# B's projections, dilated attention and A's last queries on 64x64 array tiles in one mode

## The chip, the cores and the metric

One core of a Trainium2 chip. The metric is the device time of one execution in microseconds (us). The experiments ran on three chips (e1 to e4, e5 to e11, e12). The kernel before, timed in the same rounds, took 488.0, 488.2 and 489.4 us on them (medians), so between these three groups the ratios are the safer comparison. Shares, chains and timelines come from one profiled execution of each kernel, whose span is about 2 us shorter than the time reported for it. Ratios are the mean time of one kernel's runs over that of the other's of the same rounds, so they are not quite the ratio of the medians that are quoted beside them.

## The reference, cut to what matters

Two attention blocks over the same `x` (2048 tokens, 1024 wide, 32 heads of 32) are mixed by a gate. A is linear attention. B is softmax attention in which each query sees 8 keys, two tokens apart.

```python
def _B_ref(x, wqkv, wo):
    W, dil = 8, 2
    q, k, v = ...                                  # x @ wqkv, heads of 32
    idx = pos[:, None] - (jnp.arange(W) * dil)     # even queries see even keys only, odd ones odd keys
    logits = einsum(q, k[idx]) * Dh ** -0.5        # masked where idx < 0
    return (softmax(logits) @ v[idx]) @ wo
# out = g * A(x) + (1 - g) * B(x), g = sigmoid((x * gate_w).sum(-1))
```

Tokens are held sorted by parity, so a query needs its own key and the 7 before it of the same parity.

## The kernel before, cut to what the argument touches

The middle stage, from the first projection of B's keys to the first output product, is what the change rewrites. For each of 8 head groups (128 columns, 4 heads) it makes K and Q with 64 dense matmuls of 128x128x512. In between, at fixed positions, it drops the score and PV bursts of the head group before.

```python
# dense: one matmul per k-tile, one PSUM bank per output
nc.tensor.matmul(st["pj"][:], lhsT=W[c // 4][:, kt, (c % 4) * P:(c % 4 + 1) * P],
                 rhs=xT[:, kt, cols], start=(kt == 0), stop=(kt == KT - 1))

def scores(g):            # 4 tiles of 128 keys x 112 or 128 queries, 4 heads each
    for i in range(4):    # contraction 32: one 32-row tile of the array per head
        r = slice(32 * i, 32 * i + 32)
        nc.tensor.matmul(s4[:, i, o:o + w], lhsT=kqts[c][r, 0, k0:k0 + P], rhs=kqts[c][r, 1, q0:q0 + w], ...)
    # exp on ScalarE, times mask on VectorE -> pt
def pv(g):                # 16 full 128x128 weight loads of pt, 33 columns of V (32 + a column of ones)
    nc.tensor.matmul(oB[b][:, tt - 2 * b, i, :], lhsT=pt[:, i * W_ + o:i * W_ + o + P], rhs=V[:, t, c * 4 + i, :], ...)
    # reciprocal and multiply on VectorE -> Ob, then a transposing DMA straight into OBT
...
p_ = 64 + 3 + 512 * g / len(state)          # 36 bursts, spread evenly over the dense matmuls
events.append((p_, lambda g=g: scores(g)))
events.append((p_ + 18, lambda g=g: pv(g)))
```

The output stage then sums A-side products (`pqT` with `WoA`) and B-side products (`OBT` with `WoB`) in one PSUM bank per output part.

The softmax here doesn't subtract the row's maximum and nothing guards it: scores larger than these inputs give would overflow.

## Time and profile before

| | before |
|---|---|
| time, median of 3 | 488.18 us (488.06 to 488.19) |
| TensorE busy, share of the span | 480.5 us, 99% |
| VectorE, ScalarE | 58%, 39% |
| dense matmul 128x512, start to start | 215.8 ns |
| middle stage, from its first dense matmul to the first output product | 153.5 us |
| output stage, from there to the last matmul's start | 110.8 us |

Two lines of the page of the kernel before: busy time of each engine with its share of the span and its instructions, and the chain of waits by engine.

```profile
PE 480.5 (99%) x3444; PEld 227.0 (47%) x3444; DVE 281.0 (58%) x533; ACT 187.4 (39%) x283; POOL 15.9 (3%) x33
...
PE 98%; DMA 1%; SPq 1%; ACT 0%; issue 0%; ACTq 0%
```

The chain is nearly all TensorE: nothing but less or denser TensorE work can shorten this kernel. Now one cycle of attention, from the timeline of the kernel before (start, length, engine, line, operation, count; lengths include about 0.16 us of pipeline after the last start).

```profile
301.78 0.81 PE L339 MATMUL kq_ps<-xT,WkB 128*128 128x512 bf16 x3
...
302.52 0.38 PE L365 MATMUL s<-kqt 32*128 32x128 bf16 x16
...
302.83 1.04 PE L339 MATMUL kq_ps<-xT,WkB 128*128 128x512 bf16 x4
...
303.71 0.56 PE L390 MATMUL oB<-V,PT 128*128 128x33 bf16 x16
...
304.12 0.38 PE L339 MATMUL kq_ps<-xT,WkB 128*128 128x512 bf16 x1
```

Read starts, not lengths. Three dense matmuls from 301.78 are due to end at 301.78 + 3 x 0.216 = 302.43, and the scores begin at 302.52. That is 95 ns of nothing, and 91 ns follow the last score matmul. The scores cost about 0.40 us (302.83 - 302.43) where four rounds of 49 ns, 0.2 us, would do. The PV burst, with no gap before or after it, takes 0.41 us (16 starts, 25.3 ns apart).

### The profile page before, as it was taken

Reading aid. Unit: us, or ns where it says so; the run is one execution under the profiler, and the core shown is the slowest. Engines: PE = TensorE matmul, PEld = TensorE weight load, DVE = VectorE, ACT = ScalarE, POOL = GpSimd, SP = SyncE. Lnnn points to the kernel's source line nnn. Section 1 sums busy time; section 2 is a strip of 40 time slices with the busy share of each in tenths; the row PEclk is TensorE's granted clock in tenths of the full one; section 3 lists DMA queues with packets and bytes.
Section 4 is the critical chain, followed back from the end, with each engine's and each line's share of the span. In section 5 each row is a group of like instructions: output and inputs, shape, how many; then the busy total and the mean of one; then the engine's idle time right before and its main releaser. Section 6 shows DMA issues by size and latency. Waiting matters only on the chain.

```text
span 486.2 us, 8390 instructions
## 1 busy us (share of the span) xinstructions
PE 480.5 (99%) x3444; PEld 227.0 (47%) x3444; DVE 281.0 (58%) x533; ACT 187.4 (39%) x283; POOL 15.9 (3%) x33
## 2 busy tenths in 40 slices
PE   7999999999999999999999999999999999999997
PEld 4444444445444444444444445544445444444444
DVE  1766689992429999995466556656654596000000
ACT  1333321111633333332666666666565332212121
POOL 3000001411000000000000000000000000000000
PEclk9999999999999999999999999999999999999999
DMA  8999960001522223354011161111173833111101
GB/s 194 171 291 369 348 207 0 0 1 36 190 76 93 72 71 93 95 158 131 11 30 31 30 121 27 38 30 32 31 172 78 198 88 86 34 43 34 43 33 45
DMA packets 80182, 46.57 MB, mean 96 GB/s; under 512 B 53520, under 2 KB 74128, under 8 KB 80144
## 3 DMA queue, kind: packets, MB, share of 16 engines
q1 hardware_dynamic: 80144, 46.04, 34.9%
q8 instruction: 27, 0.44, 0.4%
q14 instruction: 11, 0.09, 0.1%
HBM read 21.23 MB, written 7.34 MB: 59 GB/s over the span
## 4 chain that ended last, share of the span: by engine, by line
PE 98%; DMA 1%; SPq 1%; ACT 0%; issue 0%; ACTq 0%
PE kq_ps L339 23%; PE d_ps L454 21%; PE p_ps L258 11%; PE g_ps L200 11%; PE pk_ps L152 11%; PE p_ps L296 9%; PE q_ps L296 3%; PE oB L390 3%; PE s L365 2%; PE q_ps L454 1%; DMA WkA<-in_A_wqkv_dram 1%; PE kv_ps L220 0%; PE p_ps L246 0%; SPq L95 0%; SPq L98 0%; SPq L99 0%
## 5 line engine op out<-in xcount | busy, mean ns | idle before, releaser
L375 ACT ACTIVATE PT<-s 128x896 bf16<-128x896 f32 (+1 forms) x72 | 63.0, 926 | 24.5 <-PE s L365 24.5
L339 PE MATMUL kq_ps<-xT,WkB 128*128 128x512 bf16 x256 | 65.3, 379 | 0.0
L339 PE MATMUL kq_ps<-xT,WqB 128*128 128x512 bf16 x256 | 64.8, 379 | 0.0
L376 DVE TENSOR_TENSOR PT<-PT,mask 128x896 bf16<-128x896 bf16 (+1 forms) x72 | 44.6, 623 | 26.6 <-ACT PT L375 26.6
L258 PE MATMUL p_ps<-WvB,xT 128*128 128x512 bf16 x256 | 57.9, 379 | 0.0
L152 PE MATMUL pk_ps<-WkA,xT 128*128 128x512 bf16 x256 | 56.0, 379 | 1.3 <-DMA WkA<-in_A_wqkv_dram 0.8
L454 PE MATMUL d_ps<-WoA,pqT 128*128 128x512 bf16 (+1 forms) x248 | 56.9, 372 | 0.0
L454 PE MATMUL d_ps<-WoB,OBT 128*128 128x512 bf16 (+1 forms) x248 | 56.9, 372 | 0.0
L200 PE MATMUL g_ps<-pk,xrow 128*128 128x512 bf16 x256 | 55.4, 379 | 0.0
L140 DVE TENSOR_SCALAR e<-e 128x512 f32<-128x512 f32 x64 | 28.1, 438 | 41.8 <-ACT e L139 41.8
L459 ACT ACTIVATE osb<-d_ps,omg 128x512 bf16<-128x512 f32 (+1 forms) x31 | 20.9, 673 | 76.5 <-PE d_ps L454 73.7
L296 PE MATMUL p_ps<-WqA,xT 128*128 128x512 bf16 x192 | 43.4, 379 | 0.0
L344 ACT CAST kqt<-kq_ps 128x512 bf16<-128x512 f32 x48 | 28.2, 587 | 31.8 <-PE kq_ps L339 31.6
L152 PEld LDWEIGHTS <-xT 128*128 128x128 bf16 x256 | 24.9, 98 | 32.2 <-issue 1.6
L454 PEld LDWEIGHTS <-pqT 128*128 128x128 bf16 x264 | 25.8, 98 | 29.5
L454 PEld LDWEIGHTS <-OBT 128*128 128x128 bf16 x264 | 25.8, 98 | 29.3
L200 PEld LDWEIGHTS <-xrow 128*128 128x128 bf16 x256 | 25.0, 98 | 30.2
L258 PEld LDWEIGHTS <-xT 128*128 128x128 bf16 x256 | 24.6, 98 | 30.0 <-issue 0.9
L296 PEld LDWEIGHTS <-xT 128*128 128x128 bf16 x256 | 24.3, 98 | 28.5
L139 ACT ACTIVATE e<-pk_ps 128x512 f32<-128x512 f32 x32 | 19.0, 597 | 42.0 <-PE pk_ps L152 42.0
L339 PEld LDWEIGHTS <-WqB 128*128 128x128 bf16 x256 | 22.9, 97 | 24.7
L339 PEld LDWEIGHTS <-WkB 128*128 128x128 bf16 x256 | 22.6, 97 | 24.1
(56 smaller groups left out, 394.1 us busy)
## 6 DMA issues: line engine op xcount, KB each, us to landing
xrow<-in_A_x_dram SPq DMA_DIRECT2D x4, 1024.0 KB, 12.3
out_dram<-osb SPq DMA_DIRECT2D x31, 128.0 KB, 1.9
pqd<-tmp SPq DMA_DIRECT2D x12, 256.0 KB, 2.0
WvA<-in_A_wqkv_dram SPq DMA_DIRECT2D x2, 1024.0 KB, 15.0
WoA<-in_A_wo_dram SPq DMA_DIRECT2D x2, 1024.0 KB, 12.7
WvB<-in_B_wqkv_dram SPq DMA_DIRECT2D x2, 1024.0 KB, 12.5
WqA<-in_A_wqkv_dram SPq DMA_DIRECT2D x2, 1024.0 KB, 9.7
WkB<-in_B_wqkv_dram SPq DMA_DIRECT2D x2, 1024.0 KB, 6.6
```

The lines of the kernel that those rows point to most:

```text
L139: nc.scalar.activation(out=e[:], in_=pj[:], func=ACT.Exp)
L140: nc.vector.tensor_scalar(out=e[:], in0=e[:], scalar1=1.0, scalar2=1e-6, op0=ALU.min, op1=ALU.add)
L152: nc.tensor.matmul(pj[:], lhsT=xT[:, kt, t * P:(t + 1) * P], rhs=WkA[half][:, kt, :], start=(kt == 0), stop=(kt == KT - 1))
L200: nc.tensor.matmul(pj[:], lhsT=xrow[:, t, kt * P:(kt + 1) * P], rhs=pk[:, t, half * 512:(half + 1) * 512], start=(t == 0), stop=(t == NB - 1))
L258: nc.tensor.matmul(st["pj"][:], lhsT=xT[:, kt, t * P:(t + 1) * P], rhs=WvB[half][:, kt, :], start=(kt == 0), stop=(kt == KT - 1))
L296: nc.tensor.matmul(st["pj"][:], lhsT=xT[:, kt, t * P:(t + 1) * P], rhs=WqA[half][:, kt, :], start=(kt == 0), stop=(kt == KT - 1))
L339: nc.tensor.matmul(st["pj"][:], lhsT=W[c // 4][:, kt, (c % 4) * P:(c % 4 + 1) * P], rhs=xT[:, kt, cols], start=(kt == 0), stop=(kt == KT - 1))
L344: (nc.vector.tensor_copy if 0 <= after < 4 else nc.scalar.copy)(out=kqt[:, which, cols], in_=st["pj"][:])
L375: nc.scalar.activation(out=ptv[:, hs], in_=s4[:, hs, 0:W_], func=ACT.Exp, scale=SCALE)
L376: nc.vector.tensor_tensor(out=ptv[:, hs], in0=ptv[:, hs], in1=m[:, None, :].broadcast_to([P, 2, W_]), op=ALU.mult)
L454: nc.tensor.matmul(st["ps"][:, 0:n], lhsT=lhsT, rhs=W[c0 // 512][:, c, c0 % 512:c0 % 512 + n], start=(side == 0 and c == 0), stop=(side == ...
L459: nc.scalar.activation(out=osb[:, 0:n], in_=st["ps"][:, 0:n], func=ACT.Copy, scale=omg[:, tb:tb + 1])
```

## The change

The intent: put everything in the middle stage on 64x64 tiles, so that the array never changes mode. A dense step becomes four matmuls of 64x64x512 on the four tiles. Blocks of 64 keys replace tiles of 128. The two parities lie on the two partition halves. Scores and PV run four at a time. The exp and mask work is nearly halved. Cut to its core:

```diff
+            def quad_units(outputs):        # 4 outputs (K, Q of two parities), 4 slots of 8 steps
+                def step(slot, kt):
+                    for j in range(2):      # output half
+                        for r in range(2):  # row half
+                            o = (slot + 2 * r) % 4
+                            mm(o, r, kt, j, slot < 2)        # 64x64 weights, 512 columns
+                    if kt == KT - 1:
+                        for r in range(2):
+                            o = (slot + 2 * r) % 4
+                            if slot < 2:    # the bank goes to the other row half: a small read orders them
+                                nc.vector.tensor_copy(out=seen[:], in_=banks[o][:, 0:1])
+                            else:
+                                outputs[o][2](banks[o])
+                def evacuate(ps):           # Q twice, each with the other head of a pair zeroed
+                    if which == 0:
+                        nc.scalar.copy(out=kt_[:, par, 512 * hh:512 * hh + 512], in_=ps[:])
+                        return
+                    nc.scalar.activation(out=qz[:, 0, par, :], in_=ps[:], func=ACT.Copy, scale=qsel[:, 0:1])
+                    nc.vector.tensor_scalar(out=qz[:, 1, par, :], in0=ps[:], scalar1=qsel[:, 1:2], ...)
...
+                            nc.tensor.matmul(s2b[64 * par:64 * par + 64, pair, :, o:o + w],
+                                             lhsT=kts[c][r, par, k0:k0 + 64], rhs=qz[r, :, par, ...], ...)
...
+                                nc.tensor.matmul(o2[64 * h:64 * h + 64, par, s_, i, :], lhsT=pt[r, i, o:o + 64],
+                                                 rhs=V[r, m, 4 * c + i, :], ...)
...
-                    nc.sync.dma_start_transpose(out=OBT[:, c, q0:q0 + m * w]..., in_=Ob[0:w, t0:t0 + m]...)
+                        nc.sync.dma_start(out=obd[c][...], in_=Ob[64 * h:64 * h + w, par, sl:sl + k, :])
+                if part:
+                    nc.sync.dma_start_transpose(out=OBT[:, c, :], in_=obd[c][0:S, :])
...
+                p_ = 64 * c + (40, 52, 72, 84, 95)[m // 4]       # scores; PV 14 steps later
...
+            first = [out_part(*p_) for p_ in parts[:3]]          # A sides of 3 parts, then their B sides
+            for k in range(2):
+                for f in first:
+                    f(k)
```

V now goes to its blocks through DRAM, and the projection banks are 4 instead of 2 (6 to 4 in the first stage).

## The prediction

> **What bounds the kernel now.** TensorE: the page has PE busy 480.5 of 486.2 us, and the chain of waits is 98% PE. A dense 128x512 matmul starts every 215.8 ns. From 218 to 374 us B's projections are interrupted 36 times by attention. The trace in order of time: the 16 score matmuls (four at a time, 49 ns a set) have gaps of 95 ns before and 91 ns after them, about 0.42 us in all; the 16 PV matmuls start every 25.3 ns, 0.41 us. Together 0.83 x 36 = 29.8 us. Only this can shrink: dense work keeps its multiply-adds (576 steps of four 64x64 matmuls). VectorE (58%) and ScalarE (39%) are off the chain, so halving their exp and mask work gains nothing by itself.
>
> **What changes, costed.**
> - Dense steps. The Trainium skill, "TensorE: Matmul & The Clock Gate", Part 3, says tiles run concurrently; the trace agrees: 16 matmuls of 32x32x512 started 3.5 ns apart, all done within 0.36 us. A tile's weight load hides behind its running matmul: in the 128x64 products two tiles ran 64 columns every 31.5 ns. I expect 216 to 217 ns per step, +0.6 us over 576.
> - Mode switches. "TensorEngine Tiling (Array Packing)", Key Properties, says a mode change drains the array; the 95 and 91 ns gaps agree. One mode removes 36 x 0.19 = 7 us.
> - Scores: 8 x 18 rounds of four, 49 ns each: 7.1 us.
> - PV: twice the matmuls (1152), four at a time: 288 rounds at the 31.5 ns of the 128x64 product = 9.1 us, against 14.6.
> Attention: 16.2 instead of 29.8 us, -13.6.
>
> **What is given back (estimates).**
> - In-order queues. VectorE must mask, finish O (1.2 us a batch) and clear two Q banks (0.69 us each) before slot 1 of the next quad: about 12 us of work in each 16 us head group, one place late by 0.4 us: 8 x 0.4 = 3 us.
> - End of attention. O of the last group goes to DRAM by small writes, then one 2048x128 transpose, behind two 512x1024 transposes of pqT in the same queue (4.0 us of issue each). Last PV to landing: 1 us VectorE + 0.6 + 4 + 2.2 + 4 + 2.2 + 2 = 16 us. Cover: 18 quad steps, 24 A-side, 7 B-side matmuls = 10.7 us. TensorE idles about 5 us; the clock may drop (same page, Part 1; no idle in this trace shows it), 1 us more.
> - First stage with four banks instead of six, V through DRAM: under 1 us.
>
> Sum: 488.2 - 13.6 + 0.6 + 3 + 5 to 6 = 483; shaded to 481.5, as the positions look tuned.
>
> **Predicted: 481.5 us, 8 in 10 between 474 and 489.** Faster by over 2% (below 478.4): 0.28; within 2%: 0.67; slower: 0.05.
>
> **What would show it.** Quad matmuls: four per 216 ns. No 90 ns gaps around scores. PV bursts of 32 in about 0.25 us. PE idle on q4_ps bank releases, 2 to 4 us in all. One PE gap of about 5 us before the B-side matmul of the last group, released by the OBT transpose; lower granted clock just after.
>
> **What would make it wrong.** If weight loads (no fast load with column tiling) did not hide, steps of 240 ns or more: +14 us. PV starts limited by issue at 12 ns each: +5 us. If the last transpose landed in time: -5 us, faster by 2%. Bank releases on ScalarE later than summed: +3 to 8 us.

## The result, and the profile after

The changed kernel takes 501.25 us (median of 4 runs, 499.13 to 503.78) against 488.19. The ratio is 1.0266, with a 95% interval from 1.0228 to 1.0305: it is slower. Both the size and the direction of the forecast were wrong.

The same two lines of the page of the changed kernel:

```profile
PE 473.5 (95%) x5748; PEld 249.3 (50%) x5748; DVE 280.9 (56%) x605; ACT 167.9 (34%) x267; POOL 25.7 (5%) x88
...
PE 69%; DVE 20%; SPq 3%; ACT 3%; issue 3%; DMA 2%; ACTq 0%; DVEq 0%
```

TensorE is no longer the whole chain: VectorE has 20% of it. (Part of these 20% is the normalisation of A's queries in the first stage, to which the chain goes back from the first small read.) First, TensorE's own work, in the timeline of the changed kernel:

```profile
239.94 1.06 PE L365 MATMUL q_ps<-xT,WkB 64*64 64x512 bf16 x16
240.81 0.41 PE L418 MATMUL s2b<-qz,kt 64*64 64x114 bf16 x16
241.01 0.63 PE L365 MATMUL q_ps<-xT,WkB 64*64 64x512 bf16 x8
241.44 0.43 PE L441 MATMUL o<-V,PT 64*64 64x33 bf16 x30
```

16 small matmuls, four steps, take 240.81 - 239.94 = 0.87 us, so about 216 ns a step. The scores take 0.20 us from start to start, with no gap on either side. Single records of a PV burst show four starts every 31.5 ns. All three are what was predicted. But the stage as a whole lasts 372.30 - 218.68 = 153.6 us, as long as before. What TensorE waited for, from its list of waits (engine, tile, line, what ended the wait; us in total, times, longest):

```profile
PE d_ps L542 <- DMA OBT<-obd: 9.7, 1, 9.7
PE s2b L418 <- DVE qz L400: 5.7, 16, 0.5
PE q_ps L365 <- issue: 1.7, 1, 1.7
...
PE q_ps L365 <- DVE seen L377: 1.2, 2, 0.9
```

**Loss one, in the stage.** The work is 576 x 0.2162 + 7.1 + 9.1 = 140.7 us, so 12.9 us are lost. The last three lines above account for 8.6. That list counts idle time from the end of a matmul, and a start that waited also loses the overlap of about 0.18 us with the matmul before it (the restart, below). Counted from start to start, the 19 waits cost 12.1 us: 8.6 for `qz`, 1.6 for `seen` and 1.9 for the stop. The other 0.8 us is not explained. The commonest wait has its cause in these lines of the timeline:

```profile
235.88 1.27 ACT L399 ACTIVATE qz<-q_ps,qsel 128x512 bf16<-128x512 f32 x2 [0.65 <-PE q_ps L365]
...
236.60 1.41 DVE L400 TENSOR_SCALAR qz<-q_ps,qsel 128x512 bf16<-128x512 f32 x2 [1.01 <-ACT qz L399]
...
238.07 0.35 PE L418 MATMUL s2b<-qz,kt 64*64 64x114 bf16 x12 [0.20 <-DVE qz L400]
```

VectorE sat idle for 1.01 us and started its first copy when ScalarE's first copy (0.69 us) ended, at 236.57. It reads the same PSUM bank. The semaphores in the trace confirm it: VectorE's instruction waits for the one that ScalarE's copy raises, not for the one that TensorE raises. VectorE's own list of waits has this in all 16 places:

```profile
DVE qz L400 <- ACT qz L399: 12.8, 16, 2.7
```

So the three copies in a row, not two pairs side by side, set when the scores can start.

**Loss two, at the end of the stage.** TensorE in the timeline of the changed kernel:

```profile
377.49 1.67 PE L542 MATMUL d_ps<-WoB,OBT 128*128 128x512 bf16 x7
388.89 5.98 PE L542 MATMUL d_ps<-WoB,OBT 128*128 128x512 bf16 x17 [9.73 <-DMA OBT<-obd]
```

The DMA queue in the same timeline (start, and how long the issues held the queue):

```profile
369.54 2.66 SPq L464 DMA_DIRECT2D obd<-Ob  x5
372.30 4.91 SPq L519 DMA_TRANSPOSE pqT<-pqd  x1
377.30 2.17 SPq L464 DMA_DIRECT2D obd<-Ob  x4
379.51 4.58 SPq L519 DMA_TRANSPOSE pqT<-pqd  x1
384.32 2.48 SPq L469 DMA_TRANSPOSE OBT<-obd  x1
```

And the table by stretches of 5 us of the changed kernel (the first line names the columns):

```profile
core 0: us, PE busy (x) PEld busy (x) DVE busy (x) ACT busy (x) POOL busy (x), PEclk, DMA share, GB/s
...
380.00:385.00 5.00, 0.00 (x0) 0.00 (x0) 0.00 (x0) 0.00 (x0) 0.00 (x0) 0.80 0.98 196
385.00:390.00 5.00, 1.11 (x3) 0.43 (x4) 0.00 (x0) 0.40 (x1) 0.00 (x0) 0.50 0.66 130
390.00:395.00 5.00, 5.00 (x17) 1.96 (x16) 0.00 (x0) 1.06 (x3) 0.00 (x0) 0.67 0.16 52
```

The seven B-side products end at 377.49 + 7 x 0.216 = 379.0 and the eighth starts at 388.89: 9.9 us of nothing. The last PV burst had ended at 368.1; then the queue issued small writes, a transpose of pqT, small writes, the other transpose, and only then the transpose that TensorE needs. The granted clock fell to 0.5 in that stretch, and the next 17 products take 394.71 - 388.89 = 5.8 us instead of 3.7. Together that is 12 us, and the output stage takes 122.5 us against 110.8.

**Loss three, once.** TensorE stops for 1.67 us with no releaser ("issue"). The records of the instruction queue show why: in this stage, from 240 us on, one 16 KB fetch of instructions comes every 4.7 us on average (every 10.8 us in the kernel before, which has 1712 matmuls in the stage against 4032). The fetch just before this stop came 7.9 us after the last, behind a 1 MB load of `WoB` and two transposes. The experiments below have eight more such stops. Each ended 2.2 to 2.7 us after a late fetch began, and counted in TensorE's instructions the stops of one kernel lie whole blocks of 16 KB apart (10177 - 6593 = 14 x 256 in e3_both, 7340 - 6572 = 3 x 256 in e7_wob; 45 fetches for 11504 instructions make 64 bytes each). So TensorE had run out of instructions. A long interval alone does not show lateness: near 231 us, before attention is in full swing, TensorE uses a block more slowly, and 7.5 us pass between fetches without a stop.

### The profile page after: what moved, and what is told of

It is laid out like the page before. It is cut to its first block, busy times and chain, and to the rows that moved or that the text cites. A ratio compares the mean times of both kernels' runs of the same rounds, so it can differ in the third digit from the quotient of the medians.

```text
span 498.1 us, 13237 instructions
## 1 busy us (share of the span) xinstructions
PE 473.5 (95%) x5748; PEld 249.3 (50%) x5748; DVE 280.9 (56%) x605; ACT 167.9 (34%) x267; POOL 25.7 (5%) x88
## 4 chain that ended last, share of the span: by engine, by line
PE 69%; DVE 20%; SPq 3%; ACT 3%; issue 3%; DMA 2%; ACTq 0%; DVEq 0%
PE d_ps L542 21%; PE q_ps L365 18%; PE g_ps L201 11%; PE pk_ps L153 11%; DVE qz L400 5%; PE p_ps L276 4%; DVE tmp L141 3%; DVE tmp L293 3%; DVE den L295 3%; DVE tmp L302 3%; ACT qz L399 2%; PE s2b L418 2%; SPq L519 2%; DVE e L140 2%; PE o L441 1%
## 5 line engine op out<-in xcount | busy, mean ns | idle before, releaser
L542 PE MATMUL d_ps<-WoB,OBT 128*128 128x512 bf16 (+1 forms) x264 | 62.6, 382 | 9.7 <-DMA OBT<-obd 9.7
L365 PE MATMUL q_ps<-xT,WkB 64*64 64x512 bf16 x1024 | 70.1, 377 | 0.9 <-DVE seen L377 0.9
L365 PE MATMUL q_ps<-xT,WqB 64*64 64x512 bf16 x1024 | 63.2, 376 | 0.3 <-DVE seen L377 0.3
L542 PE MATMUL d_ps<-WoA,pqT 128*128 128x512 bf16 (+1 forms) x264 | 60.3, 373 | 0.0
L423 ACT ACTIVATE PT<-s2b 128x928 bf16<-128x928 f32 (+4 forms) x40 | 34.2, 855 | 56.2 <-PE s2b L418 56.2
L425 DVE TENSOR_TENSOR PT<-PT,mask 128x928 bf16<-128x928 bf16 (+4 forms) x40 | 23.6, 590 | 34.6 <-ACT PT L423 34.6
L365 PEld LDWEIGHTS <-WqB 64*64 64x64 bf16 x1024 | 33.6, 107 | 16.5 <-issue 0.9
L153 PEld LDWEIGHTS <-xT 128*128 128x128 bf16 x256 | 24.9, 98 | 32.8 <-issue 2.2
L276 PEld LDWEIGHTS <-xT 128*128 128x128 bf16 x256 | 24.7, 98 | 30.0 <-issue 0.9
L365 PEld LDWEIGHTS <-WkB 64*64 64x64 bf16 x1024 | 30.7, 107 | 14.0 <-issue 1.8
L281 ACT CAST tmp<-p_ps 128x512 bf16<-128x512 f32 x32 | 18.7, 589 | 37.4 <-PE p_ps L276 32.6
L312 PEld LDWEIGHTS <-xT 128*128 128x128 bf16 x192 | 18.8, 98 | 22.6
```

The lines of the kernel that those rows point to most:

```text
L153: nc.tensor.matmul(pj[:], lhsT=xT[:, kt, t * P:(t + 1) * P], rhs=WkA[half][:, kt, :], start=(kt == 0), stop=(kt == KT - 1))
L276: nc.tensor.matmul(st["pj"][:], lhsT=xT[:, kt, t * P:(t + 1) * P], rhs=WvB[half][:, kt, :], start=(kt == 0), stop=(kt == KT - 1))
L312: nc.tensor.matmul(st["pj"][:], lhsT=xT[:, kt, t * P:(t + 1) * P], rhs=WqA[half][:, kt, :], start=(kt == 0), stop=(kt == KT - 1))
L365: nc.tensor.matmul(banks[o][64 * j:64 * j + 64, :], lhsT=lhsT(r, kt, j), rhs=rhs(r, kt), start=first and kt == 0, stop=kt == KT - 1, skip_ ...
L423: nc.scalar.activation(out=pt[:, :, 0:W_], in_=s2b[:].rearrange("p a b s -> p (a b) s")[:, :, 0:W_], func=ACT.Exp, scale=SCALE)
L425: nc.vector.tensor_tensor(out=pt[:, :, 0:W_], in0=pt[:, :, 0:W_], in1=mask[:, None, base:base + W_].broadcast_to([P, 4, W_]), op=ALU.mult)
```

## The experiments

Twelve kernels were run. All gave the right result. "Stage" is the middle stage and "output" the output stage, both from the timeline of the one profiled run.

| kernel | time, us | ratio to before, 95% | stage | output |
|---|---|---|---|---|
| before | 488.19 | 1 | 153.5 | 110.8 |
| changed | 501.25 | 1.0266 (1.0228 to 1.0305) | 153.6 | 122.5 |
| e1_evac | 496.07 | 1.0163 (1.0127 to 1.0199) | 145.6 | 125.3 |
| e2_tail | 495.79 | 1.0136 (1.0087 to 1.0184) | 153.0 | 118.2 |
| e3_both | 489.31 | 1.0026 (1.0001 to 1.0051) | 148.3 | 115.3 |
| e4_warm | 500.02 | 1.0243 (1.0213 to 1.0272) | 153.3 | 120.3 |
| e5_cover | 482.16 | 0.9868 (0.984 to 0.9896) | 147.1 | 110.5 |
| e6_dense | 496.74 | 1.017 (1.0147 to 1.0194) | 158.7 | 112.5 |
| e7_wob | 483.01 | 0.989 (0.9869 to 0.9911) | 147.0 | 110.5 |
| e8_all | 480.62 | 0.9848 (0.9823 to 0.9874) | 146.2 | 110.5 |
| e9_pieces | 484.16 | 0.9921 (0.9881 to 0.996) | 146.8 | 110.5 |
| e10_place | 482.81 | 0.9886 (0.985 to 0.9922) | 147.5 | 110.5 |
| e11_swap | 489.88 | 1.0034 (1.0011 to 1.0057) | 146.6 | 117.8 |
| e12_two | 479.03 | 0.9792 (0.9773 to 0.9811) | 144.4 | 110.5 |

The start of the stage wanders from 218.4 to 220.5 us among these profiled runs, with the waits for the first loads of the first stage. In six of them (e2, e3, e4, e5, e7, e12) the clock also stood at 0.5 for 3.4 us near 8 us, and these are the six that start after 219.8. So single spans are not compared below 2 us.

### e1_evac: Q cleared bank by bank

```diff
-                    nc.scalar.activation(out=qz[:, 0, par, :], in_=ps[:], ..., scale=qsel[:, 0:1])
-                    nc.vector.tensor_scalar(out=qz[:, 1, par, :], in0=ps[:], scalar1=qsel[:, 1:2], ...)
+                    for slot in range(2):
+                        if par == 1:
+                            nc.scalar.activation(out=qz[:, slot, par, :], in_=ps[:], ..., scale=qsel[:, slot:slot + 1])
+                        else:
+                            nc.vector.tensor_scalar(out=qz[:, slot, par, :], in0=ps[:], scalar1=qsel[:, slot:slot + 1], ...)
```

> Only the clearing of Q changes: ScalarE makes both masked copies of one Q bank and VectorE both of the other, instead of each engine making one copy of each bank. Theory A (the two engines may not read one PSUM bank together, so VectorE's copies start only after ScalarE's, and TensorE waits for a chain of about 2.1 us where 1.4 us would do): TensorE's waits for VectorE's qz, 5.7 us in 16 waits of 0.24 or 0.47 us, shrink below 1 us, each also saves its pipeline refill of about 0.16 us, and the time falls by 6 to 10 us, to about 491 to 495. Rival B (the placement of the score bursts or the total of VectorE's work sets the wait): the same work in the same place, the waits stay within 1 us of 5.7 us and the time within 2 us of 501.

The timeline of e1_evac, at the same place of a later head group:

```profile
252.08 1.41 DVE L404 TENSOR_SCALAR qz<-q_ps,qsel 128x512 bf16<-128x512 f32 x2 [0.40 <-PE q_ps L365]
252.09 1.27 ACT L401 ACTIVATE qz<-q_ps,qsel 128x512 bf16<-128x512 f32 x2 [0.70 <-ACT kt L397]
```

Two lines of TensorE's list of waits in e1_evac:

```profile
PE d_ps L546 <- DMA OBT<-obd: 13.0, 1, 13.0
PE s2b L422 <- DVE qz L404: 1.5, 7, 0.2
```

The engines now copy side by side, the waits fell from 5.7 to 1.5 us (I had expected under 1), and the stage from 153.6 to 145.6 us. About 2 us of that is the late fetch, which this run did not have; the other 6 are the 4.2 us of waits and their restarts. Theory A held for the stage. The time fell by only 5.2 us, about 1 us short of the range expected: the wait at the end grew from 9.7 to 13.0 us, because TensorE reached the output stage 7.4 us earlier, but the last transpose was issued only 4.1 us earlier (380.20 against 384.32). A gain in the stage is partly given back at a later wait until that wait is gone too.

### e2_tail: the last transpose first

```diff
             for r0 in (512, 1024):
+                nc.vector.tensor_copy(out=pqT[2][:, 0, r0 - 512:r0 - 511], in_=OBT[:, KT - 1, 0:1])
                 nc.sync.dma_start_transpose(out=pqT[2][:, :, r0 - 512:r0], in_=pqd[r0:r0 + 512, :])
```

The added copies make the two large transposes depend on the arrival of `OBT`. Without such a dependency they go ahead of it, as in the changed kernel, where they are written after it too.

> Only the queue order at the end of attention changes: the two 512x1024 transposes of pqT are made to wait for the transpose of the last head group. Theory A (queue order: they stand ahead of it and hold the queue 4.9 and 4.6 us): the one TensorE gap of 9.7 us shrinks to 0 to 1.5 us, the granted clock stays at 1.0, and the time falls by 10 to 12 us, to about 489 to 491. Rival B (the small writes to DRAM, their landing and the transpose itself are the long part): the gap shrinks by less than 4 us.

The wait at the end in TensorE's list of waits of e2_tail:

```profile
PE d_ps L543 <- DMA OBT<-obd: 5.2, 1, 5.2
```

Its DMA queue, from the timeline:

```profile
371.75 6.76 SPq L464 DMA_DIRECT2D obd<-Ob  x9
380.72 1.76 SPq L469 DMA_TRANSPOSE OBT<-obd  x1
385.47 8.04 SPq L520 DMA_TRANSPOSE pqT<-pqd  x2
```

The time fell by 5.5 us, half of what I expected: neither theory alone. The queue order was worth 4.5 us of the wait. The other half is the path itself: nine small writes hold the queue for 6.8 us, the transpose waits 2.2 us for them to land (378.51 to 380.72), and the product that waits for it starts 4.5 us after its issue began. In this profile the clock still fell (the 17 products took 6.1 us), where I had expected it to stay. One of the four timed runs, at a mean clock of 1.0, took 491.31 us, almost what theory A said. No profile fell on it, so how its wait differed is not known.

### e3_both: both edits

> Both edits. If the two losses are separate and add up: 501 less 6 to 10 less 10 to 12, so 479 to 485, faster than the kernel before by 1 to 2%. If they overlap (quads that end earlier leave less cover for the tail), the gain is 3 us or more short of the sum of the two single gains.

489.31 us: 11.9 us gained, where the single gains add up to 10.6. The losses are separate and add up. It still does not beat the kernel before (ratio 1.0026, from 1.0001 to 1.0051), and it missed the 479 to 485 expected because e2_tail gained half of what I expected and e1_evac a little less. A wait of 3.0 us for `OBT` is left.

### e4_warm: the idle stretch filled with useless matmuls

```diff
+            spare = ps_pj.tile([P, 512], F32, name="spare", tag="pj")
+            for i in range(44):
+                nc.tensor.matmul(spare[:], lhsT=xT[:, 0, 0:P], rhs=WoA[0][:, 0, :], start=True, stop=True)
```

> 44 matmuls of no use (9.5 us) are put in the gap before the last B-side products, so that TensorE does not idle there. The result stays right. Theory A (the idle time lets the clock drop, and the products after it run at a lower clock for about 5 us): the granted clock stays at 1.0 and the time falls by about 2 us although nothing useful was added. Rival B (the lower clock costs nothing or comes from something else): same time within 0.5 us, or the clock drops all the same.

In the profiled run the clock stays at 1.0 from 11 us on. The 17 products after the wait:

```profile
389.91 3.84 PE L542 MATMUL d_ps<-WoB,OBT 128*128 128x512 bf16 x17 [0.22 <-DMA OBT<-obd]
```

They take 393.59 - 389.91 = 3.7 us instead of 5.8, and the output stage is 120.3 us against 122.5: 2.2 us less, the whole slow part. In the timed runs the gain is 1.2 us (500.02 against 501.25, with overlapping intervals), so they alone do not settle it. The traces do: the same wait without idling costs nothing afterwards. The Trainium skill, "TensorE: Matmul & The Clock Gate", Part 1, describes this gate: an idle window of about 3.4 us brings half clock until TensorE has been busy for as long. The trace agrees roughly, with 0.5 in a stretch where TensorE hardly ran and 2.2 us lost after it. A shorter stretch was enough, though: 3.0 us of idle time in e3_both brought 3.4 us at half clock, while 2.1 us in e6_dense brought none.

### e5_cover: more independent work ahead of the last transpose

```diff
-            first = [out_part(*p_) for p_ in parts[:3]]
+            AHEAD = 7          # four more banks, free after attention
+            first = [out_part(*p_, *((ps_pj, "pj") if i < 3 else (ps_3, "d3"))) for i, p_ in enumerate(parts[:AHEAD])]
```

This is e3_both with 7 A sides, 12.1 us of matmuls, ahead of the first B side.

> e3_both with the A-side products of seven output parts instead of three ahead of the first B-side product (four more PSUM banks, free after attention): 32 matmuls, 6.9 us more cover for the last transpose. Theory A (what is left of the tail is latency that more independent work hides): the gap of 3.0 us and the dip of the clock vanish, 3 to 4.5 us less than e3_both of the same kind of run, about 485 to 486.5. Rival B (the transpose is held up by other traffic and lands later still): a gap of over 1 us stays.

482.16 us. The wait for `OBT` is gone from the list and the output stage is 110.5 us. Before, that stage held one PV burst of 0.41 us as well, so it is now exactly the dense work of the kernel before. Theory A held. The gain over e3_both, 7.2 us, is more than the 3 to 4.5 expected: 4.8 us of it is the output stage (115.3 to 110.5) and 1.2 us the middle stage, where this run lists 0.9 us of late fetch instead of 1.9. The two profiled runs differ by just 5.5 us. The medians differ by more because three of e5_cover's four runs had a mean clock of 1.0, and none of e3_both's had.

### e6_dense: dense steps back on 128x128, attention left on 64x64

```diff
-                    for j in range(2):
-                        for r in range(2):
-                            mm(o, r, kt, j, slot < 2)
+                    nc.tensor.matmul(st["ps"][:], lhsT=lhsT(kt), rhs=rhs(kt), start=kt == 0, stop=kt == KT - 1)
```

This is e3_both otherwise. It undoes the one mode and nothing of the attention.

> e3_both with the dense steps put back to 128x128 matmuls, attention left on 64x64 tiles. Theory A (the change of mode costs about 95 ns each way, as in the kernel before, and one mode removes it): 40 score bursts and 40 PV bursts, each with 0.19 us of switching, +15 us of TensorE time, less 1.5 to 3 us of waits for the reads that order the halves and the Q banks: 12 to 14 us slower than e3_both, about 501 to 503. Rival B (four matmuls of 64x64 cost more per step than one of 128x128, so the dense steps lose what the switches gain): within 4 us of e3_both.

The timeline of e6_dense around one score burst and one PV burst:

```profile
256.83 1.03 PE L361 MATMUL q_ps<-xT,WkB 128*128 128x512 bf16 x4
257.79 0.40 PE L407 MATMUL s2b<-qz,kt 64*64 64x114 bf16 x16
258.34 0.38 PE L361 MATMUL q_ps<-xT,WkB 128*128 128x512 bf16 x1 [0.16 <-issue]
258.65 0.43 PE L430 MATMUL o<-V,PT 64*64 64x33 bf16 x32
```

The switches are back: 95 ns before the scores (257.69 to 257.79), and 0.55 us from their start to the next dense matmul where one mode needs 0.20. The stage is 158.7 us against 148.3, so 10.4 us longer, although e6_dense has none of e3_both's waits for `qz` and `seen`. The timed runs are 7.4 us slower than e3_both, below the 12 to 14 expected, but far from B's "within 4"; 2.8 us of the stage's loss come back in the output stage (112.5 against 115.3), where the wait for `OBT` is shorter. So the one mode is worth at least 10 us of the stage. It was not the mode that made the changed kernel slow.

### e7_wob, e8_all: the load moved, the first small reads moved

```diff
-            WoB = load_w("WoB", B_wo, 0, "wb")
+            WoB = load_w("WoB", B_wo, 0, "wb", only=(0,)) + load_w("WoB", B_wo, 0, "wc", only=(1,))
```

> e5_cover with the second half of WoB loaded about 256 steps earlier into a buffer that is free by then, out of the stretch in which TensorE waited 1.1 to 1.7 us with nothing that released it. Theory A (TensorE runs dry there because a fetch of its instructions, one every 4.4 us in the quads, stands behind the 1 MB load and the transposes): the gap disappears or falls below 0.3 us, fetches there stay under 6 us apart, 1 to 2 us faster than e5_cover. Rival B (the transposes of pqT alone hold up the fetch): the gap stays at 1 us or more.

483.01 us, no faster than e5_cover. The stop at the old place (0.87 us in the profiled run of e5_cover) is gone, but a new one stands at 299.6 us, behind the load at its new place (issued at 291.5 us), where two fetches came 7.6 us apart. So A's mechanism holds and its gain does not: I had only moved the load, and put 2 MB in a row.

e8_all adds, for the first quad, the small reads on ScalarE:

```diff
-                                nc.vector.tensor_copy(out=seen[:], in_=banks[o][:, 0:1])
+                                (nc.scalar.copy if early else nc.vector.tensor_copy)(out=seen[:], in_=banks[o][:, 0:1])
```

> e7_wob, and the four small reads that order the row halves in the first quad are made by ScalarE, because VectorE is still normalising A's queries there. The waits of 0.9 and 0.3 us on these reads go, with their refills 1.5 us: about 481.5 to 484, 1% faster than the kernel before. If the waits only move to the Q banks of the first quad, which VectorE clears, less than 0.5 us is gained.

480.62 us, 1.5% faster than before, a little better than expected; the waits for `seen` are gone from the list. In its timeline the late fetch is plainer still (two fetches 8.5 us apart):

```profile
294.89 0.81 PE L365 MATMUL q_ps<-xT,WkB 64*64 64x512 bf16 x10
297.44 0.62 PE L365 MATMUL q_ps<-xT,WkB 64*64 64x512 bf16 x6 [1.73 <-issue]
```

TensorE stops in the middle of a dense output, after 10 of 16 matmuls, where no data is awaited.

### e9_pieces, e10_place: two misses

e9_pieces is e8_all with `WoB` in 16 pieces of 128 KB that ScalarE issues over the last four head groups.

```diff
+                    nc.scalar.dma_start(out=WoB[h][:, kt, :], in_=B_wo[kt * P:(kt + 1) * P, 512 * h:512 * h + 512])
+                    events.append((64 * c + (5, 18, 37, 50)[i], wo_event(c, i)))
```

> e8_all with WoB fetched in 16 pieces of 128 KB, spread over the last four head groups and issued by ScalarE at set places, instead of 2 MB at once. Theory A (a fetch of TensorE's instructions is late wherever a big load stands before it): no fetch of the quads comes over 6 us after the one before, no TensorE gap without a releaser in the quads, about 1.5 us faster than e8_all, 479 us. Rival B (the late fetch has another cause): a gap of 0.7 us or more stays. A risk: ScalarE holds back its copies while it waits to issue a piece; then waits for its copies appear on TensorE.

No fetch came over 5.9 us after the one before, and no stop without a releaser is left in the quads: A's mechanism again. But the time rose to 484.16 us: the risk named came true, with 0.9 us of new waits for ScalarE's `PT` in the profiled run. Three of the six timed runs were at 481.7 to 482.8 us, and three at 485.5 to 486.4 with a lower mean clock (0.993). No profile fell on one of the slower three, so what happened in them stays open.

e10_place moves the last score burst of each head group two steps on.

```diff
-                p_ = 64 * c + (40, 52, 72, 84, 95)[m // 4]
+                p_ = 64 * c + (40, 52, 72, 84, 97)[m // 4]
```

> e9_pieces with the last score burst of each head group two dense steps later, so that its mask no longer stands before the clearing of Q on VectorE. The waits for VectorE's qz (1.5 us in 7 waits of 0.2 us) disappear, with their refills about 2.5 us: 476.5 to 478 us, over 2% faster than the kernel before. If they only move to ScalarE or to the bank releases, less than 1 us.

482.81 us, against 476.5 to 478 expected. The waits for `qz` are gone, and 3.0 us in three waits for ScalarE's copies of K appeared: the wait only moved, as the second half of the expectation says.

### e11_swap: each engine still one copy of each bank, in crossed order

```diff
+                    act(0, pa, psa)      # ScalarE on the one bank, VectorE on the other,
+                    dve(1, pb, psb)
+                    act(0, pb, psb)      # then they change
+                    dve(1, pa, psa)
```

> e3_both, but with each engine making one copy of each Q bank, as in the changed kernel, only in such an order that the two are never due on one bank at once (ScalarE begins with the one bank, VectorE with the other, then they change). It tells two readings of e1_evac apart. Theory A (what cost the time was that both engines had to take turns on one bank): the same as e3_both within 1 us, and the stage from the first quad to the first output product within 1 us of its 148.3 us. Rival B (the split of the work by bank did it, for instance because one semaphore wait fewer is on the way): the stage is back near 153 us.

The two engines at the first pair of copies, and TensorE's wait for `qz`, in e11_swap:

```profile
235.65 1.51 ACT L408 ACTIVATE qz<-q_ps,qsel 128x512 bf16<-128x512 f32 x2 [0.65 <-PE q_ps L365]
235.68 1.44 DVE L412 TENSOR_SCALAR qz<-q_ps,qsel 128x512 bf16<-128x512 f32 x2 [0.33 <-PE q_ps L365]
...
PE s2b L434 <- ACT qz L408: 1.9, 7, 0.3
```

VectorE now starts when TensorE releases it. The stage is 146.6 us and the time 489.88, against 148.3 and 489.31 for e3_both. The stage falls outside the 1 us band on the better side, as this run had no late fetch (e3_both listed 1.9 us). The time does not follow, as the wait for `OBT` is 5.8 us against 3.0. The copies and their split between the engines are those of the changed kernel, only never both engines on one bank at once: the gain is there. It was the turns on one bank.

### e12_two: `WoB`'s second half in two pieces

This is e8_all with two issues of 512 KB instead of 1 MB straight after the first.

```diff
+            for i in range(2):
+                events.append((64 * (5 + i) + 46, wo_event(i)))    # ScalarE, 4 k-tiles each
```

> e8_all with the second half of WoB in two pieces of 512 KB, issued by ScalarE in the sixth and seventh head groups at a place where it has nothing due, instead of 1 MB straight after the first half. Theory A (the fetch of instructions was 8.5 us after the one before it because 2 MB stood in front of it): no interval over 6.5 us, no gap without a releaser over 0.5 us, no new waits for ScalarE (two issues instead of sixteen), 1 to 1.7 us faster than e8_all: 479 to 479.6 us. If ScalarE's waits for its own issues cost as much as in e9_pieces, no faster than e8_all.

479.03 us, ratio 0.9792 (from 0.9773 to 0.9811). All that TensorE waits for in e12_two:

```profile
PE s2b L422 <- DVE qz L404: 1.5, 7, 0.2
PE pk_ps L153 <- DMA WkA<-in_A_wqkv_dram: 1.2, 2, 1.1
PE warm L159 <- DVE onesb L110: 1.1, 1, 1.1
PE pk_ps L153 <- DMA xT<-in_A_x_dram: 0.5, 1, 0.5
```

From 240 us on the longest interval between fetches is 5.6 us, and no stop without a releaser is left in the stage. The time is in the range expected. This version beats both kernels. The interval reaches past 0.98, so "faster by over 2%" stays unclear, "faster" does not.

## Why the prediction was wrong, point by point

- **Bound, dense steps, mode, scores, PV: right.** The dense step measured 216 ns (predicted 216 to 217), scores 0.20 us a burst without gaps, PV four per 31.5 ns. e6_dense shows that the mode is worth 10 us or more. The fear about weight loads did not come true. e12_two's stage is 144.4 us against 153.5 before: of the 13 us predicted as TensorE work saved, 9 can be had.
- **The step that failed first: "one place late by 0.4 us: 8 x 0.4 = 3 us".** It measured 8.6 us, of the 12.9 lost in the stage. The prediction had dense matmuls wait for VectorE to release banks, and no such wait is listed; the scores waited for `qz`. I let ScalarE and VectorE clear Q side by side. They share a bank and took turns, so the scores were late in 16 places, not 8, and each wait cost a restart of about 0.18 us as well. e1_evac took about 6 us off the stage with this alone, and e11_swap shows that the turns were the cause. The Trainium skill has the rule behind this: "PSUM — Partial Sum Buffer", section "PSUM bank collisions raise a hardware error", has any two engines kept off one bank on the same partitions, reads included. I had not looked it up for two readers. No run here lets them collide; what the trace shows is VectorE kept waiting for ScalarE's copy, 12.8 us of its idle time in 16 places.
- **The small reads that order the row halves were not costed at all** in the sum. They cost 1.2 us of waits (1.6 us from start to start), only in the first quad, where VectorE was still normalising A's queries. e8_all removed them.
- **The second failed step: "TensorE idles about 5 us; the clock may drop ..., 1 us more".** The mechanism was right, in order, queue and clock. The size was 9.9 and 2.2 us. From the last PV to landing I added up 16 us; it took about 20.8 (368.1 to 388.9). The cover was right: 10.9 us of work against 10.7. The path was not: the writes ahead of the first large transpose held the queue 2.7 us, where the sum has 0.6, and the large transposes took 4.9 and 4.6 us of issue, not 4.0. The queue was also still busy with earlier transposes when the last PV ended. e2_tail and e5_cover show that the order and the lack of cover were each about half of it.
- **Missing from the prediction: the instruction fetch**, 1.7 us in the profiled run. It moved with the load (e7_wob, e8_all) and went when the load was cut (e9_pieces, e12_two). But e1_evac and e11_swap, with the load as it was, had no late fetch either. So the load makes a late fetch possible, not certain, and what decides it is open.
- **The shading "as the positions look tuned" was no evidence** and went the wrong way.

In the sum of the prediction, 483 to 484 us, the two mis-sized terms add 8.6 - 3 = 5.6 and 12 - 5.5 = 6.5 us, and the two missing ones 1.6 and 1.9 us. That gives 499 to 500, and the profiled run took 499.8.

So where did the gain go? TensorE's 13 us of saved work was spent, inside the stage, mostly on waits for a VectorE that is itself idle for over a third of it (busy 95.5 of 153.8 us); and 12 us more were lost once, at the seam to the next stage, where the new way of O through DRAM is longer than the work that covers it.

## What to carry to other kernels

When TensorE is made denser, write down for each PSUM bank who reads it and when: two engines that share one bank add their times, and a crossed order cost nothing here. At a seam between stages sum up the whole path of the last tile, with everything that stands before it in its DMA queue, and compare it with the independent work that covers it; an idle stretch is paid again in clock. More and smaller matmuls also need more instructions fetched, and a large load in one piece in front of a fetch can hold it up.

## What the Trainium skill lacked or had wrong

- "Runtime: NRT & Kernel Launch", "Instruction fetch mechanics", calls the cost of crossing a 16 KiB block "mostly hidden". It has no word of other DMA traffic: here a fetch that came 7.9 or 8.5 us after the one before, where one comes every 4.5 to 4.7 us on average, stopped TensorE for 1.7 us. The page gives both 128 KiB for TensorE (2048 instructions) and a memory of only two 16 KiB lines. In e8_all TensorE stopped 513 matmuls and weight loads after the last fetch before the late one, two blocks of 256, which fits the small figure.
- "TensorE: Matmul & The Clock Gate", Part 3, says that weight loads overlap running matmuls "only when row_grp differs", though the page elsewhere also allows a load into a background buffer. In the kernel before, each weight load of a full 128x128 array (98 ns) starts 2 ns after the start of a matmul on all rows, and matmuls still follow each other every 215.8 ns.
- "TensorEngine Tiling (Array Packing)" gives no time for a change of mode (95 and 91 ns around the 32-row scores) and does not say that four 64x64x512 matmuls a step, each with its own weight load, keep the pace of one 128x128x512 (216 ns against 215.8).
- "DMA: Bandwidth & Descriptors" has a cycle count for issuing a DMA transpose of small tiles and a bandwidth, but no page gives the time for which larger ones hold their queue: 3.7 to 5.6 us for 512x1024 here and 1.7 to 3.6 us for 2048x128, with two longer ones (5.6 and 6.5) in e6_dense.
